# Score tiles set apart, q and k turned together, and x of batch 3 turned by transfers, in a kernel of attention and an MLP

## The chip, the cores and the metric

The kernel runs on one core of one Trainium2 chip. The metric is device time in microseconds (us); three runs of the kernel before took 359.74, 359.81 and 360.06 us, median 359.81. The engines are named as in the profile: PE is the matrix engine, PEld its weight loads, DVE the vector engine, ACT the scalar engine with its activation functions, POOL the general-purpose engine, SP the engine that only issues transfers here.

## What is computed

The reference is attention with a decay ("forgetting attention"), followed by an MLP. There are 8 batches of 8 heads; a sequence has 576 positions and a head 64 elements.

```python
scores = scale * np.matmul(q, k.transpose(0, 1, 3, 2))
cum = np.cumsum(np.log(np.clip(f, 0.0001, 1.0)), axis=-1)
scores = np.where(causal, -1e9, scores + cum[..., :, None] - cum[..., None, :])
attn = softmax(scores)                       # over the last axis
x = np.matmul(attn, v)                       # then (B, S, H*D) -> 4608 x 512
h = x @ w_in                                 # 512 x 2048
out = (h * 1 / (1 + np.exp(-h))) @ w_out     # 2048 x 512
```

Inputs and output are float32; the matrix products run in bfloat16.

## The kernel before, in words

**Attention.** A *pair* is two heads of one batch; there are four pairs per batch and 32 in all, numbered p = 0 to 31. `scores(p, t)` makes one of four tiles (t = 0 to 3) of the transposed scores of a pair: keys on the partitions, queries along the row, only the part at or below the diagonal. Both heads use 64 rows of PE each (64 is the head's size). A score tile `sc` lies in one of two PSUM buffers; ACT takes the exponential of it into `uT`. The diagonal blocks must be masked. In the first four pairs a large negative number is added to the score tile before the exponential, by DVE, or for tile 2 by PE; later DVE multiplies the exponentials with zeros and ones. The decay does not enter the scores: v, and a column of ones beside it, are multiplied by `wT`, a function of the running sum of log f, by POOL in `prep_v` (result `vaug`, three buffers). `attend_rows(p)` multiplies `uT` with `vaug` on PE (30 matmuls of 65 columns, called row sums in this text), and DVE divides by the column that sums the weights (`rr`, `xt`).

**Getting q and k to lie with the head's elements on the partitions.** Batches 0 and 1, and q of batch 2, come as float32 (`whole`, `raw`), are cast by POOL (`cast_both`), transposed by PE (`transposes`, tile `tpqk`) and copied by DVE. Everything later is loaded by POOL's queue with a cast (`load_qk`, tile `mp`), one block of 128 positions of q or k at a time, and transposed by a transfer issued on SP (`turn_qk`).

**Turning x.** The MLP needs x with its 512 columns on the partitions. For batches below `NTURN` = 4, `turn_pair` transposes a pair's x on PE (five transposes, tile `tpx`; the last has 64 rows) and ACT copies it to `xT` (two copies per pair). For the other batches `retire` puts five turns of a whole block by transfer (`turn_batch`, on SP) on a list, due 2.5 to 7.3 units of the planner's clock later.

**The MLP.** Tokens are taken in nine groups of 512. `m1_chunk` makes a 128-row slice of the first layer (four matmuls of 512 columns, tile `hp`), then ACT's tanh (`th`) and DVE's product (`gtile`), 16 per group. `m2_part` is a quarter of an output tile of the second layer (four matmuls, tile `po`); the fourth quarter is followed by ACT's copy (`osb`) and a store. These chunks and parts are called parts below. Part n of an output tile reads the n-th quarter of w_out, and the four quarters are loaded by POOL in this order after `prep_v` of pair 4.

**What sets the order.** Every engine runs its instructions in the order in which this Python code issues them. A loop over pairs 4 to 31 issues each pair's scores, the row sums of the pair before, loads and turns by a table (`plan`, `fetch`), and n parts, given by `pace`: what is ready, spread over the pairs until the next group will be ready, with `LAG` (10) in units of time for the wait at the batch's end and at most `MOST` = 9. `work(n)` takes parts from the two queues; `spend` moves the planner's clock, and what was put off with `defer` is issued when the clock has passed its time. Before pair 4 the order is written out by hand; after pair 31 the rest of the MLP follows without a pause.

The lines that matter below are 270 to 320 (`scores`), 337 to 377 (row sums and turns of x by PE), 379 to 438 (turns by transfer, the MLP), 484 to 539 (pace, retire, tables) and 594 to 701 (the order by hand and the loop).

Of the kernel before, what the change touches and what calls it, by code (L numbers as in the profile page):

```python
# [13 lines left out]
FP32 = mybir.dt.float32  # L14
BF16 = mybir.dt.bfloat16
P = 128
# [3 lines left out]
def kernel(  # L20
# [29 lines left out]

    const = ctx.enter_context(tc.tile_pool(name="const", bufs=1))
    ident_bf = const.tile([P, P], BF16, name="ident_bf")
    ident_f = const.tile([P, P], FP32, name="ident_f")
# [6 lines left out]
    vaugs = [const.tile([P, NB, 2, DV], BF16, name=f"vaug{i}") for i in range(NVA)]  # L60
    kTs = [const.tile([P, NPB, NB * P], BF16, name=f"kT{i}") for i in range(2)]
# [3 lines left out]
    qkp = ctx.enter_context(tc.tile_pool(name="qkp", bufs=2))  # L65
    vp = ctx.enter_context(tc.tile_pool(name="vp", bufs=2))
# [8 lines left out]
    RAW = {0: (0, 1), 1: (0, 1), 2: (0,)}  # L75
    NTURN = 4
    LAG = 10.0
    MOST = 9.0
# [5 lines left out]
    def qk_tiles(b):  # L84
        qkT[b] = (qkp.tile([P, NPB, S], BF16, name="qT", tag="qT"), kTs[b % 2])

# [36 lines left out]
    def load_qk(b, c, which):  # L123
        t = sbp.tile([P, DM], BF16, name="mp", tag="mp", bufs=16)
        raw[b, c, which] = t
        nc.gpsimd.dma_start(  # L126
            out=t[: bs[c], :].rearrange("p (h d) -> p h d", h=H),
            in_=(q, k)[which][b, :, c * P : c * P + bs[c], :].rearrange("h p d -> p h d"),
        )

    def turn_qk(b, c, which):
        if b not in qkT:
            qk_tiles(b)
        n = bs[c]
        nc.sync.dma_start_transpose(
            out=qkT[b][which][:, :, c * P : c * P + n], in_=raw[b, c, which][:n, :]
        )
# [16 lines left out]
    def decay_sum():  # L154
        lnf = f_sb
        cum = evp.tile([BH, S], FP32, name="cum", tag="ev")
        nc.vector.tensor_tensor_scan(
            out=cum[:, :], data0=lnf[:, :], data1=lnf[:, :], initial=0.0,
            op0=ALU.add, op1=ALU.bypass,
        )  # L160
        mid = const.tile([BH, 1], FP32, name="mid")
        nc.vector.tensor_scalar_mul(out=mid[:, :], in0=cum[:, S - 1 : S], scalar1=0.5)
        cumc = cum
        nc.vector.tensor_scalar(
            out=cumc[:, :], in0=cum[:, :], scalar1=mid[:, 0:1], scalar2=None,
            op0=ALU.subtract,
        )
        cums.append(cumc)

    cums: list = []  # L170
# [35 lines left out]
    def turn_first(which):  # L206
        qk_tiles(0) if 0 not in qkT else None
        m = cast[0, 0, which].rearrange("p c h d -> p c (h d)")
        tp = big([P, SM], BF16, "tpqk")
        for c in range(NB - 1):  # L210
            nc.tensor.transpose(tp[:, c * P : (c + 1) * P], m[:, c, :], ident_bf[:, :])
        nc.vector.tensor_copy(
            out=qkT[0][which][:, 0, 0:SM].rearrange("x (p c) -> x p c", c=NB - 1),
            in_=tp[:, :].rearrange("x (c p) -> x p c", c=NB - 1),
        )

# [53 lines left out]
    def scores(p, t):  # L270
        qT, kT = (x[:, p % NPB, :] for x in qkT[p // NPB])
        u = us[p % 3]
        first = p < NPB
        sc = psc.tile([P, 2, 512], FP32, name="sc", tag="sc")
# [209 lines left out]
    def pace(p):  # L484
        b, j = divmod(p, NPB)
        if b < NEARLY:
            return have() / (NPB - j)
        for b in range(B):
            if (b + 1) * S // TG > m1_ready:
                break  # L490
        n = MOST
        for _ in range(20):
            k = NPB * (b + 1) - p + min(LAG, 3.5 * (b - 1)) / (2.3 + 0.88 * n)
            n = 0.5 * n + 0.5 * have() / max(k, 1.0)
        return min(n, MOST)
# [10 lines left out]
    def retire(p):  # L506
# [3 lines left out]
        for c in range(NB):  # L510
            defer(2.5 + 1.2 * c, lambda c=c: turn_batch(b, c))
        for g in range(b * S // TG, (b + 1) * S // TG):
# [10 lines left out]
    for b in range(NEARLY, B):  # L523
        for i, group in enumerate([(0, 1), (2,), (3, 4)]):
            at = NPB * b - 4 + min(i, 1) if b == NEARLY else NPB * b - 7 + i
            late = 1 if b == NEARLY + 1 and len(RAW[NEARLY]) == 2 else 0
            for c in group:
                for w in range(2):
                    if w in RAW.get(b, ()):
                        continue  # L530
                    add(fetch, at + late, load_qk, b, c, w)
                    if b <= NEARLY + 1:
                        to = min(at + late + (2 if b == NEARLY else 3), NPB * b - 2)
                        add(plan, to, turn_qk, b, c, w)
                    elif i == 0 and b - 2 >= NTURN:
                        add(plan, NPB * b - 4, defer, 9.0, partial(turn_qk, b, c, w))
                    else:
                        add(plan, NPB * b - 4 + min(i, 1), turn_qk, b, c, w)
                add(plan, NPB * b - 5 + i + (b == NEARLY), load_v, b, c, nc.sync)
# [11 lines left out]

    with tc.manual_schedule():
        nc.scalar.dma_start(out=f_sb[:, :], in_=f.rearrange("b h s -> (b h) s"))
        load_main(0, 0, 2)
# [17 lines left out]
        make_identity(nc, ident_f)  # L572
        for kT in kTs:
            nc.vector.memset(kT[:, :, S:], 0.0)
        for u in us:
# [17 lines left out]
        load_w(w_in_bf, moe_w_in, DFF // 2, DFF)  # L593
        for w in range(2):
            turn_first(w)
        scores(0, 0)
        turn_first_tails()
        scores(0, 1)
        decay_sum()
        scores(0, 3)  # L600
        transposes(1, 0)
        scores(0, 2)
        decay_turn()
        prep_v(0)
        transposes(1, 1)
        scores(1, 0)
        cast_both(3)
        load_tail(1)
# [4 lines left out]
        for p in range(1, NPB):  # L613
# [3 lines left out]
            if more:  # L617
                transposes(p + 1, 0)
            scores(p, 3)
            if more:  # L620
                transposes(p + 1, 1)
            if p > 1:
                turn_pair(p - 2)
            attend_rows(p - 1, LO)
            scores(p, 2)
# [20 lines left out]
        for p in range(NPB, NP):  # L646
# [6 lines left out]
            due -= n  # L653
            n1, n2 = (n + 2) // 3, (n + 1) // 3
            n3 = n - n1 - n2
            scores(p, 0)
            scores(p, 1)
            spend(0.4)
            work(n1)
            ahead = RAW.get((p + 1) // NPB, ())  # L660
            rows = NPB < p < NPB * NEARLY
            if 0 in ahead:
                transposes(p + 1, 0)
# [71 lines left out]
```

## Time and profile before

| | |
|---|---|
| three runs | 359.74, 359.81, 360.06 us |
| profiled execution | 359.25 us, of which the profile's span is 357.5 |
| PE | 336.3 us busy, 94% |
| ACT | 211.9 us, 59% |
| DVE | 191.7 us, 54% |
| POOL | 119.6 us, 33% |
| first layer (`hp`) | 135.8 us of PE, second layer (`po`) 133.7 |
| row sums (`avr`) | 36.2 us of PE, 960 matmuls |
| scores (`sc`) | 37.3 us of PE, 384 matmuls, 2 to 8 at a time |
| x transposed by PE (`tpx`) | 64 matmuls of 128 rows and 16 of 64 |

The page has the busy time of each engine, rows of 40 slices of the span, the queues, the chain of work that ended last, and the costliest groups with what ended the idle time before them. A timeline's line gives start, duration, engine, source line, operation, tiles and count; where there was an idle time before it of which the end is known, it stands in brackets with its releaser. A matmul's duration is longer than its place in the stream, since matmuls overlap; what a step costs is read from starts. The table by stretch gives the length of the stretch, busy time and count of PE, PEld, DVE, ACT and POOL, the granted clock, the share of the transfer engines, and GB/s. Some matmul records are missing, so a count can be one or two too low.

### The profile page before, as it was taken

The page shows a single profiled execution, that of the slowest core. Times are in us where ns is not written, and L with a number is a line of the kernel's source. Part 1 is how long each engine was busy: PE and PEld are TensorE (multiplying, and loading weights), DVE is VectorE, ACT ScalarE, POOL GpSimd, SP SyncE. Part 2 cuts the span into 40 slices and gives each one's busy share as a digit, 9 for nine tenths or more (in the row PEclk, how much of TensorE's full clock was granted, in tenths as well). Part 3 has the DMA queues.
Part 4 walks back from the last instruction along what each step waited for, and adds up shares of the span by engine and source line. Part 5 has one row for each costly group of instructions (what it writes and reads, how often), then busy time and mean ns, then how long its engine had stood idle before and what let it go on. Part 6 is the DMA issues. An engine that isn't in the chain of part 4 may idle for free.

```text
span 357.5 us, 7026 instructions
## 1 busy us (share of the span) xinstructions
PE 336.3 (94%) x2656; PEld 168.4 (47%) x2697; DVE 191.7 (54%) x450; ACT 211.9 (59%) x345; POOL 119.6 (33%) x207
## 2 busy tenths in 40 slices
PE   2797989999999999999999999999999999999995
PEld 1455445554555445544454453444444454444442
DVE  4664895538743675348543791567237723744300
ACT  4566674558753986388647764676468615644421
POOL 5563598239554235423564250110301000000000
PEclk9999999999999999999999999999999999999999
DMA  8899999999997998399969994452240014000021
GB/s 220 213 208 315 192 193 222 155 210 170 148 150 117 163 150 78 89 170 142 124 122 152 130 166 123 100 117 75 74 83 31 1 68 118 2 29 29 31 76 71
DMA packets 142514, 44.92 MB, mean 126 GB/s; under 512 B 129616, under 2 KB 136784, under 8 KB 142480
## 3 DMA queue, kind: packets, MB, share of 16 engines
q1 hardware_dynamic: 87664, 33.64, 42.5%
q0 software_dynamic: 54736, 10.69, 38.4%
q8 instruction: 21, 0.34, 0.4%
q10 hardware_dynamic: 80, 0.15, 0.2%
q14 instruction: 13, 0.11, 0.1%
HBM read 36.85 MB, written 9.44 MB: 129 GB/s over the span
## 4 chain that ended last, share of the span: by engine, by line
PE 82%; DVE 6%; ACT 4%; DMA 3%; issue 3%; POOL 1%; SPq 0%; ACTq 0%
PE po L425 33%; PE hp L400 30%; PE avr L349 7%; PE sc L281 7%; DVE gtile L412 2%; ACT uT L306 2%; DMA xT<-xt 2%; PE tpx L371 2%; DVE uT L320 2%; PE tpqk L235 2%; ACT th L411 1%; DMA whole<-in_k_dram 1%; DVE xt L359 1%; PE sc L289 1%; DVE qT L240 1%
## 5 line engine op out<-in xcount | busy, mean ns | idle before, releaser
L400 PE MATMUL hp<-xT,w_in_bf 128*128 128x512 bf16 x556 | 135.8, 380 | 3.2 <-DVE gtile L412 0.8
L425 PE MATMUL po<-w_out_bf,gtile 128*128 128x512 bf16 x555 | 133.7, 379 | 1.4 <-DVE gtile L412 0.4
L412 DVE SCALAR_TENSOR_TENSOR gtile<-th,hp 128x512 bf16<-128x512 bf16 x144 | 96.0, 685 | 52.2 <-ACT th L411 50.3
L306 ACT ACTIVATE uT<-sc 128x1024 bf16<-128x1024 f32 (+1 forms) x128 | 101.3, 850 | 24.9 <-PE sc L281 15.9
L411 ACT ACTIVATE th<-hp 128x512 bf16<-128x512 f32 x144 | 84.8, 613 | 50.0 <-PE hp L400 46.2
L251 POOL TENSOR_TENSOR vaug<-vm,wT 128x512 bf16<-128x512 f32 x64 | 45.4, 729 | 132.7 <-PE avr L349 121.4
L400 PEld LDWEIGHTS <-w_in_bf 128*128 128x128 bf16 x576 | 53.1, 98 | 65.2 <-issue 6.1
L425 PEld LDWEIGHTS <-gtile 128*128 128x128 bf16 x576 | 53.6, 98 | 62.9 <-issue 2.4
L320 DVE TENSOR_TENSOR uT<-uT,mask 128x256 bf16<-128x256 bf16 (+1 forms) x112 | 35.3, 337 | 66.2 <-ACT uT L306 66.0
L434 ACT ACTIVATE osb<-po 128x512 f32<-128x512 f32 x36 | 21.7, 602 | 46.7 <-PE po L425 46.7
L281 PE MATMUL sc<-qT,kT 64*128 64x64 bf16 (+4 forms) x384 | 37.3, 287 | 5.5 <-ACT uT L306 2.2
L349 PEld LDWEIGHTS <-uT 128*128 128x128 bf16 x960 | 33.7, 98 | 6.4 <-issue 0.7
L349 PE MATMUL avr<-vaug,uT 128*128 128x65 bf16 x960 | 36.2, 195 | 0.2 <-POOL vaug L259 0.2
L359 DVE TENSOR_TENSOR xt<-avr,rr 128x384 bf16<-128x384 f32 x64 | 31.4, 491 | 2.3
L281 PEld LDWEIGHTS <-kT 64*128 64x128 bf16 x384 | 15.3, 95 | 30.1 <-issue 21.0
L126 POOL DMA_DIRECT2D mp<-in_k_dram x30 | 25.9, 865 | 1.0 <-DMA mp<-in_k_dram 1.0
L126 POOL DMA_DIRECT2D mp<-in_q_dram x25 | 22.2, 887 | 1.3 <-DMA w_out_bf<-in_moe_w_out_dram 0.5
L358 DVE RECIPROCAL rr<-avr 128x6 f32<-128x6 f32 x64 | 11.7, 183 | 18.6 <-PE avr L349 18.5
L377 ACT COPY xT<-tpx 128x512 bf16<-128x512 bf16 (+7 forms) x32 | 11.2, 404 | 17.0 <-PE tpx L371 16.9
L193 POOL CAST m<-whole 128x512 bf16<-128x512 f32 x20 | 11.9, 607 | 15.0 <-DMA whole<-in_q_dram 12.4
L235 PE MATMUL tpqk<-ident_bf,m 128*128 128x128 bf16 (+1 forms) x90 | 10.9, 241 | 0.3 <-DVE gtile L412 0.3
L235 PEld LDWEIGHTS <-m 128*128 128x128 bf16 (+1 forms) x90 | 7.3, 106 | 6.3 <-issue 1.6
(47 smaller groups left out, 71.8 us busy)
## 6 DMA issues: line engine op xcount, KB each, us to landing
out_dram<-osb SPq DMA_DIRECT2D x36, 256.0 KB, 2.2
vm<-in_v_dram SPq DMA_DIRECT2D x32, 256.0 KB, 4.7
mp<-in_k_dram POOLq DMA_DIRECT2D x24, 128.0 KB, 6.2
whole<-in_q_dram SPq DMA_DIRECT2D x5, 512.0 KB, 9.7
mp<-in_q_dram POOLq DMA_DIRECT2D x20, 128.0 KB, 4.8
w_in_bf<-in_moe_w_in_dram POOLq DMA_DIRECT2D x2, 1024.0 KB, 11.2
w_out_bf<-in_moe_w_out_dram POOLq DMA_DIRECT2D x4, 512.0 KB, 10.7
whole<-in_k_dram SPq DMA_DIRECT2D x3, 512.0 KB, 9.5
```

Of the source, the lines that this page charges most:

```text
L126: nc.gpsimd.dma_start(out=t[: bs[c], :].rearrange("p (h d) -> p h d", h=H), in_=(q, k)[which][b, :, c * P : c * P + bs[c], :].rearrange("h ...
L235: nc.tensor.transpose(tp[:, c * P : c * P + n], m[:n, c, :, :].rearrange("p h d -> p (h d)"), ident_bf[:n, :n],)
L251: nc.gpsimd.tensor_tensor(out=va[:n, c0:c1, :, 0:D], in0=vm[:n, c0:c1, 2 * j : 2 * j + 2, :], in1=wT[:n, c0:c1, 2 * j + b * H : 2 * j + 2 ...
L281: nc.tensor.matmul(sc[:, i, col : col + n], lhsT=kT[r, kb * P : (kb + 1) * P], rhs=qT[r, q0 : q0 + n], start=True, stop=not pe_adds,)
L306: nc.scalar.activation(out=u[:, :, o : o + col], in_=sc[:, :, 0:col], func=ACT.Exp, scale=scale)
L320: nc.vector.tensor_tensor(out=d, in0=d, in1=mk, op=ALU.mult)
L349: nc.tensor.matmul(av[:, qb - lo, i, :], lhsT=u[:, i, o : o + P], rhs=va[:, kb, i, :], start=(kb == 0), stop=(kb == qb),)
L359: nc.vector.tensor_tensor(out=xt[:, lo:hi, 2 * j : 2 * j + 2, :], in0=av[:, :, :, 0:D], in1=r[:, 0:n, :, None].to_broadcast([P, n, 2, D]), ...
L400: nc.tensor.matmul(hp[:, :], lhsT=w_in_bf[:, cc, fc * P : (fc + 1) * P], rhs=xg[g][:, cc, :], start=(cc == 0), stop=(cc == NCC - 1),)
L411: nc.scalar.activation(out=th[:, :], in_=hp[:, :], func=ACT.Tanh, scale=0.5)
L412: nc.vector.scalar_tensor_tensor(out=gte[:, fc, :], in0=th[:, :], scalar=1.0, in1=hp[:, :], op0=ALU.add, op1=ALU.mult,)
L425: nc.tensor.matmul(po[:, :], lhsT=gte[:, fc, tb * P : (tb + 1) * P], rhs=w_out_bf[:, fc, :], start=(fc == 0), stop=(fc == NFC - 1),)
```

## The change

1. `scores` adds the mask before the exponential in pairs 4 and 5 too, except in tile 2.
2. In the loop, the parts of a pair stand in other places: in batches 1 and 2 some stand between any two of the four score tiles; later two tiles still follow each other, with a third of the parts behind the first two. (`step` keeps the count.)
3. q and k of a batch share one buffer, and one transfer turns a block of both (8 x 128 columns where there were two of 4 x 128). The loads of a block of q and k share one tile, of which there are eight.
4. x of batch 3 is turned by transfers (`NTURN` 3), and the turns of a batch are issued at once behind its last row sums, ahead of what SP is given next.
5. `LAG` is 14, and from the batch at which transfers begin it is no longer shortened, so more parts are kept for the wait at a batch's end.
6. Ahead of the row sums of pair 0, 34 matmuls of a zero tile (`spin`) stand between PE's other work; the first copy of k is made in two pieces.

```diff
-    NTURN = 4
-    LAG = 10.0
+    NTURN = 3
+    LAG = 14.0
...
-    def turn_qk(b, c, which):
+    def turn_qk(b, c):
...
         nc.sync.dma_start_transpose(
-            out=qkT[b][which][:, :, c * P : c * P + n], in_=raw[b, c, which][:n, :]
+            out=qkTs[b % 2][:, w[0] :, :, c * P : c * P + n].rearrange(
+                "x w j n -> x (w j) n"
+            ),
+            in_=raw[b, c][:n, w[0] * DM :],
         )
...
+    def spin(n):
+        ps = big([P, SM], FP32, "spin")
+        for _ in range(n):
+            nc.tensor.matmul(
+                ps[:, :], lhsT=idle[:, 0:P], rhs=idle[:, :], start=True, stop=True
+            )
...
-        nc.vector.tensor_copy(
-            out=qkT[0][which][:, 0, 0:SM].rearrange("x (p c) -> x p c", c=NB - 1),
-            in_=tp[:, :].rearrange("x (c p) -> x p c", c=NB - 1),
-        )
+        dst = qkT[0][which][:, 0, 0:SM].rearrange("x (p c) -> x p c", c=NB - 1)
+        for p0, p1 in ((0, P),) if which == 0 else ((0, P // 4), (P // 4, P)):
+            nc.vector.tensor_copy(
+                out=dst[:, p0:p1, :],
+                in_=tp[:, :].rearrange("x (c p) -> x p c", c=NB - 1)[:, p0:p1, :],
+            )
...
-        first = p < NPB
+        first = p < NPB + 2 and (t != 2 or p < NPB)
...
-            k = NPB * (b + 1) - p + min(LAG, 3.5 * (b - 1)) / (2.3 + 0.88 * n)
+            k = NPB * (b + 1) - p + (LAG if b >= NTURN else min(LAG, 3.5 * (b - 1))) / (2.3 + 0.88 * n)
...
         for c in range(NB):
-            defer(2.5 + 1.2 * c, lambda c=c: turn_batch(b, c))
+            turn_batch(b, c)
...
-        for w in range(2):
-            turn_first(w)
+        spin(7)
+        turn_first(0)
+        spin(4)
+        turn_first(1)
+        spin(2)
         scores(0, 0)
         turn_first_tails()
+        spin(2)
         scores(0, 1)
+        spin(3)
...
-            n1, n2 = (n + 2) // 3, (n + 1) // 3
-            n3 = n - n1 - n2
-            scores(p, 0)
-            scores(p, 1)
-            spend(0.4)
-            work(n1)
+            scores(p, 0)
+            spend(0.3)
+            step(0.2 if b <= NEARLY else 0.0)
+            scores(p, 1)
+            spend(0.3)
+            step(0.2 if b <= NEARLY else 0.35)
...
-            if early:
-                work(n2 // 2)
+            step(0.1 if b <= NEARLY else 0.0)
             scores(p, 2)
+            spend(0.3)
+            step(0.2 if b <= NEARLY else 0.0)
             scores(p, 3)
-            spend(0.3)
+            spend(0.2)
...
+            step(0.1)
             if rows:
                 attend_rows(p - 1, HI)
-            work(n2 - n2 // 2 if early else n2)
+            step(0.0 if b <= NEARLY else 0.25)
             if b >= NEARLY and j > 0:
                 attend_rows(p - 1)
                 spend(1.2)
-            work(n3)
+            work(left)
```

More of the change, by code (lines that the diff above doesn't have):

```diff
@@ L51 @@
     const = ctx.enter_context(tc.tile_pool(name="const", bufs=1))
+    idle = const.tile([P, SM], BF16, name="idle")
     ident_bf = const.tile([P, P], BF16, name="ident_bf")
@@ L60 @@
     vaugs = [const.tile([P, NB, 2, DV], BF16, name=f"vaug{i}") for i in range(NVA)]
-    kTs = [const.tile([P, NPB, NB * P], BF16, name=f"kT{i}") for i in range(2)]
+    qkTs = [const.tile([P, 2, NPB, NB * P], BF16, name=f"qkT{i}") for i in range(2)]
     us = [const.tile([P, 2, UW], BF16, name=f"uT{i}") for i in range(3)]
     xp = ctx.enter_context(tc.tile_pool(name="xp", bufs=4))
-    qkp = ctx.enter_context(tc.tile_pool(name="qkp", bufs=2))
     vp = ctx.enter_context(tc.tile_pool(name="vp", bufs=2))
@@ L84, in qk_tiles @@
     def qk_tiles(b):
-        qkT[b] = (qkp.tile([P, NPB, S], BF16, name="qT", tag="qT"), kTs[b % 2])
+        qkT[b] = (qkTs[b % 2][:, 0], qkTs[b % 2][:, 1])
     def raw_tile():
@@ L123, in load_qk @@
     def load_qk(b, c, which):
-        t = sbp.tile([P, DM], BF16, name="mp", tag="mp", bufs=16)
-        raw[b, c, which] = t
+        if (b, c) not in raw:
+            raw[b, c] = sbp.tile([P, 2 * DM], BF16, name="mp", tag="mp", bufs=8)
         nc.gpsimd.dma_start(
-            out=t[: bs[c], :].rearrange("p (h d) -> p h d", h=H),
+            out=raw[b, c][: bs[c], which * DM : (which + 1) * DM].rearrange(
+                "p (h d) -> p h d", h=H
+            ),
             in_=(q, k)[which][b, :, c * P : c * P + bs[c], :].rearrange("h p d -> p h d"),
         )
-    def turn_qk(b, c, which):
+    def turn_qk(b, c):
         if b not in qkT:
@@ L134, in turn_qk @@
         n = bs[c]
+        w = [x for x in range(2) if x not in RAW.get(b, ())]
         nc.sync.dma_start_transpose(
-            out=qkT[b][which][:, :, c * P : c * P + n], in_=raw[b, c, which][:n, :]
+            out=qkTs[b % 2][:, w[0] :, :, c * P : c * P + n].rearrange(
+                "x w j n -> x (w j) n"
+            ),
+            in_=raw[b, c][:n, w[0] * DM :],
         )
@@ L528 @@
                 for w in range(2):
[L529 to L538, printed above, removed]
+                    if w not in RAW.get(b, ()):
+                        add(fetch, at + late, load_qk, b, c, w)
+                if b <= NEARLY + 1:
+                    to = min(at + late + (2 if b == NEARLY else 3), NPB * b - 2)
+                else:
+                    to = NPB * b - 4 + min(i, 1)
+                add(plan, to, turn_qk, b, c)
                 add(plan, NPB * b - 5 + i + (b == NEARLY), load_v, b, c, nc.sync)
@@ L552 @@
     with tc.manual_schedule():
+        nc.vector.memset(idle[:, :], 0.0)
         nc.scalar.dma_start(out=f_sb[:, :], in_=f.rearrange("b h s -> (b h) s"))
@@ L572 @@
         make_identity(nc, ident_f)
-        for kT in kTs:
-            nc.vector.memset(kT[:, :, S:], 0.0)
+        for t in qkTs:
+            nc.vector.memset(t[:, 1, :, S:], 0.0)
         for u in us:
@@ L593 @@
         load_w(w_in_bf, moe_w_in, DFF // 2, DFF)
-        for w in range(2):
-            turn_first(w)
+        spin(7)
[3 more added lines that the diff above has]
+        spin(2)
         scores(0, 0)
         turn_first_tails()
+        spin(2)
         scores(0, 1)
+        spin(3)
         decay_sum()
         scores(0, 3)
+        spin(1)
         transposes(1, 0)
+        spin(2)
         scores(0, 2)
+        spin(1)
         decay_turn()
@@ L605 @@
         transposes(1, 1)
+        spin(4)
         scores(1, 0)
+        spin(2)
         cast_both(3)
@@ L618 @@
                 transposes(p + 1, 0)
+            if p == 1:
+                spin(2)
             scores(p, 3)
@@ L623 @@
                 turn_pair(p - 2)
+            else:
+                spin(4)
             attend_rows(p - 1, LO)
@@ L653, with step @@
             due -= n
-            n1, n2 = (n + 2) // 3, (n + 1) // 3
-            n3 = n - n1 - n2
-            scores(p, 0)
-            scores(p, 1)
-            spend(0.4)
-            work(n1)
             ahead = RAW.get((p + 1) // NPB, ())
             rows = NPB < p < NPB * NEARLY
+            left, part = n, 0.0
+            def step(share):
+                nonlocal left, part
+                part += share * n
+                k = min(left, int(part + 0.5))
+                part -= k
+                left -= k
+                work(k)
+            scores(p, 0)
[4 more added lines that the diff above has]
+            step(0.2 if b <= NEARLY else 0.35)
             if 0 in ahead:
```

## The prediction

> **What bounds the kernel now.** I read the page first: TensorE (PE) is busy 94% of a span of 357.5 us, and the chain that ended last is 82% PE. Then the busy time by stretch, to see where the other 6% lies.
>
> ```profile
> PE 336.3 (94%) x2656; PEld 168.4 (47%) x2697; DVE 191.7 (54%) x450; ACT 211.9 (59%) x345; POOL 119.6 (33%) x207
> DMA  8899999999997998399969994452240014000021
> ```
> ```profile
> 0.00:35.00 35.00, 24.20 (x256) 14.40 (x258) 19.39 (x58) 19.74 (x30) 18.95 (x47) 1.00 0.99 238
> 35.00:57.50 22.50, 20.55 (x151) 10.17 (x152) 19.71 (x39) 14.71 (x24) 17.49 (x31) 1.00 1.19 194
> 57.50:100.00 42.50, 40.98 (x360) 21.49 (x365) 25.36 (x63) 28.47 (x49) 23.00 (x37) 1.00 1.66 177
> 150.00:340.00 190.00, 187.75 (x1377) 90.37 (x1398) 100.99 (x223) 115.18 (x184) 38.54 (x62) 1.00 0.55 90
> ```
>
> PE idles 10.8 us of the first 35, 2.0 of the next 22.5, and then 4.5 up to 340. The second line is the DMA row: nine tenths and more from the second slice to past 60 us, so the front is paced by transfers too. Behind 57 us there is little waiting to win, and what an edit adds to PE's stream is paid almost in full.
>
> Two lines of the front matter: when POOL issued the w_out loads, and when PE used them (timelines of POOL and PE; then landings of the issue at 43.6, with its neighbour).
>
> ```profile
> 39.85 1.40 POOL L251 TENSOR_TENSOR vaug<-vm,wT 128x512 bf16<-128x512 f32 x2 [4.49 <-DMA vm<-in_v_dram]
> 41.33 3.03 POOL L542 DMA_DIRECT2D w_out_bf<-in_moe_w_out_dram  x4
> 57.33 0.88 POOL L126 DMA_DIRECT2D mp<-in_q_dram  x1 [0.52 <-DMA w_out_bf<-in_moe_w_out_dram]
> ...
> 56.12 2.76 PE L425 MATMUL po<-w_out_bf,gtile 128*128 128x512 bf16 x12
> ...
> DMA to landing us min/median/max: 11.7/12.6/13.5
> ```
>
> The fourth load, issued at 43.6, lands 13.5 us later, at 57.1; POOL, which waits for that queue, goes on at 57.33. PE starts the part that reads it eight matmuls into the last PE line: 56.12 + 8 x 0.216 = 57.85. So only about 0.6 us lies between landing and use.
>
> Third, what a step in PE's stream costs (PE timeline in four narrow windows).
>
> ```profile
> 116.62 0.38 PE L400 MATMUL hp<-xT,w_in_bf 128*128 128x512 bf16 x1
> 116.84 0.38 PE L425 MATMUL po<-w_out_bf,gtile 128*128 128x512 bf16 x1
> ...
> 118.35 0.38 PE L400 MATMUL hp<-xT,w_in_bf 128*128 128x512 bf16 x1
> 118.66 0.31 PE L281 MATMUL sc<-qT,kT 64*128 64x320 bf16 x2
> ...
> 150.74 0.52 PE L371 MATMUL tpx<-ident_bf,xt 128*128 128x128 bf16 x5
> 151.06 0.63 PE L281 MATMUL sc<-qT,kT 64*128 64x512 bf16 x6
> ```
>
> From one 128-row matmul to the next the starts lie 0.22 apart (hp to po), but from a 128-row matmul to a 64-row score matmul 0.31. A change of row count costs 0.10, as long as the score's weight load (95 ns in its group). Leaving costs the same: the last 64-column score pair to the next hp takes 0.12, where pairs inside follow within 0.03. Five transposes of a pair end in a 64-row one, so scores behind them pay nothing more: tpx to sc is 0.32.
>
> **The change part by part.** An "MLP part" is four matmuls, 4 x 0.216 = 0.865.
>
> Front (spins, the k copy in two, the memset). 34 spin matmuls stand ahead of the first row sums, seven of them in the 4.51 us before PE's first work. Five transposes took 0.78 at 16.79 and 0.52 at 38.65, a ratio of 0.67, though the granted clock reads 1.00 in both. If the spins bring the quick matmuls on early, the other 27 cost 5.8 us, against 4.25 of waits between 4.51 and 17.74 and a third (2.9) off the 8.6 us of work there: they fit. If they don't, they cost 27 x 0.216 x 1.5 = 8.8, or 4.5 us too much. I take the first, since PE became fast at 22 after 4.2 us without a gap. The Trainium skill, "TensorE: Matmul & The Clock Gate", Part 1, says that an idle array runs at half rate and is released after about 3.4 us of activity; no run here yet shows it for spins. Row sums of pair 0 still wait for POOL's vaug (17.69), which hangs on transfers alone. From there to 21.98 the sluggish matmuls took 4.24 us; a third off gives 1.4. The split copy (0.18 for 64 columns, 0.69 for 512; I take 0.3 for its first piece) and the memset (0.17 to 0.33 on an idle DVE) lie ahead of that wait and count nothing.
>
> Masks of pairs 4 and 5 added before the exponential. Two masks of pair 4 took 2.09 beside a busy POOL, the adds cost 0.43 each and 0.28 for the small one; DVE's queue then lets kT go sooner. Of the 1.95 us that PE idles from 35 to 57.5 I count 1.7 as gone (bounds 0 and 1.95). Setting score tiles apart adds eight changes of row count in pairs 4 and 5, 0.8. So PE would reach that last w_out part 1.4 + 1.7 - 0.8 = 2.3 us sooner, at 55.55. But the load lands at 57.1 to 57.3: its issue hangs on prep_v(4), that on the v loads at 39.85, those on transfers and POOL, none of them changed. PE waits, and **0.6** is what remains.
>
> Score tiles set apart in pairs 6 to 11. Counted in the order of both built programs, changes of row count in these pairs go from 34 to 64: two more places per pair where parts stand between two tiles, and transposes that led straight into scores now lead into a part. 30 x 0.096 = **+2.9**, all on PE, in a stretch where PE waited 1.5 us. Later pairs keep two tiles together and gain none.
>
> The Trainium skill, same page, "Step-by-step: what each phase is for", has PE pull weight loads ahead of running matmuls when row groups don't conflict or a background buffer takes them, and gives 128 columns / 1.2 GHz = 107 ns for one. An estimate by that price is 3.2 instead of 2.9; an estimate by the pulling ahead is nothing, the first rival below. The trace agrees with the pulling ahead from 128 rows to 128 rows (0.22) and not from 128 to 64 (0.31).
>
> Batch 3's x turned by transfers. Four times five transposes go: three that led into scores save 0.32 - 0.10 = 0.22 each, one that led into row sums 0.45 (147.64 to 148.09): **-1.1**. ACT loses eight copies of 0.40, beside PE. SP gains six turns of 1.24; group 3 needs three of them, so 3 x 1.24 + 2.4 to 4.9 landing = 6.1 to 8.6 after the last row sums. Cover: seven MLP parts (6.05), two pairs' scores (1.9), one pair's row sums (0.9) = 8.9. Hidden; if that cover is gone, each late us costs one.
>
> x turns at once, q and k together. Turns stand ahead of the next q/k turns, v loads and output stores on SP, which wait up to 1 us for DVE plus 6.2 us of issue; four osb buffers cover two stores. The q/k issues go from 55 to 30; the wide one costs between 1.2 and 2.4 us of SP, I take 1.9, a batch ahead of use: nothing. At groups 4 and 5 PE had waited 0.3 and 0.3 for xT; the turns now start some 3 us sooner, -0.6. POOL's loads wait for q/k turns of one batch earlier (eight double buffers for sixteen): those landed before 75, hidden.
>
> Waits otherwise. The 0.44 for gtile at 85.68 goes with parts spread finer, -0.4. Pair 12 now has four first-layer parts and one second-layer part: ACT 3 x 1.03 + 0.30 + 4 x 0.61 + 0.60 = 6.4 against PE's 5.4; before, 7.7 against 7.2. Scores of pair 13 wait for it: +0.6 beside the 0.33 at 128.43. Transposes of pairs 6, 9 and 10 have one part (0.865) between row sums and themselves where there were two or three; with none, at 76.86, PE waited 0.55, so +0.4 in all. The 0.52 for an exponential at 191.61 (a pair with one part) moves to pair 17. Net 0; bounds -1 to +1.5.
>
> Sum: -0.6 + 2.9 - 1.1 + 0 = +1.2. The profiled execution took 359.25 (span 357.5 and 1.75 around it), which gives 360.45; the median of the runs shown is 359.81, 0.56 above it, so **361.0**.
>
> **The rivals.**
> - Changes of row count cost nothing when a part stands between tiles, because the score weights are loaded while the part runs. For it: 128-row loads are hidden that way. The Trainium skill's sentence on weight loads, above, would allow it too. Against it: every hp or po to sc step I read is 0.31. Price: the 2.9 goes, 359.81 - 1.7 = 358.1. It decides if a change costs under 0.03; above 0.08 the kernel is slower.
> - The load wall doesn't stand: w_out lands 2 us sooner and 2.3 instead of 0.6 come through, 359.81 - 0.5 = 359.3. Against it: a DMA row at nine tenths up to there, and unchanged queues.
> - Waits grow: ACT binds in pairs 12 to 14 and the transposes wait for DVE in each early pair, +1.5: 362.5. For it: ACT's 6.4 against 5.4.
> - Spins change nothing in that: 4.5 late and the 1.4 not gained; 4.5 - 1.7 + 0.8 = 3.6 late past the wall, with +1.8 behind it 365.2. Against it: 22 us.
>
> **How the numbers follow.** Forecast 0.50 (own range 360.2 to 361.9), row changes free 0.12, no wall 0.14, waits grow 0.17, spins in vain 0.07. About 0.2% (0.7 us) is what a measurement can tell from no change: faster is under 359.1, slower over 360.5. Faster: free changes 0.12 and most of no wall 0.08, 0.20. Same: the rest of no wall and the forecast's lower end, 0.18. Slower 0.62. The range leaves out the free changes and the vain spins: 359.0 to 362.9.
>
> **What the profile after would show.** Transposes at 0.52 for five from before 10 us; row sums of pair 0 still at about 17.7; a PE wait on w_out near 55 to 57; hp to sc still 0.31, and pair 8 to 11 longer by 0.4 to 0.6 each; no tpx after pair 11; hp of group 3 without a wait for xT. Wrong would be: no wait on w_out, score tiles entered at 0.22, or PE idling over 1 us in pairs 12 to 17.

## The result, and the profile after

The changed kernel took 362.61 us (median of six runs, 362.28 to 364.40); the kernel before, run beside it, took 359.77 (six runs, 359.22 to 360.87). The ratio is 1.0084, with a 95% interval of 1.0059 to 1.0109: slower by about 3 us. The profiled execution took 362.71 us, of which the span is 360.5; the prediction's sum for it was 360.45.

The page of the changed kernel: PE is busy for longer, and one slice has a clock below full.

```profile
PE 344.7 (96%) x2668; PEld 166.3 (46%) x2711; DVE 192.4 (53%) x452; ACT 209.6 (58%) x337; POOL 120.3 (33%) x207
PEclk9999989999999999999999999999999999999999
```

Busy time says little here, since matmuls at half the clock count as busy (1.71 of the 2.00 us from 50 on, below), and the spins count too. What tells is where each pair's first score tile starts on PE. All columns but the first are differences to it, from one profiled execution of each kernel; e1 to e11 are the experiments below.

| start of | before, us | after | e1 | e2 | e3 | e4 | e6 | e8 | e9 | e11 |
|---|---|---|---|---|---|---|---|---|---|---|
| pair 4 | 42.26 | -1.88 | -2.23 | -1.80 | -2.26 | -1.58 | -0.58 | -0.71 | -1.83 | -0.73 |
| pair 5 | 50.16 | +0.13 | -2.25 | -1.56 | -2.71 | -0.50 | -0.46 | -0.51 | -2.11 | +1.55 |
| pair 6 | 59.04 | +1.41 | -1.09 | +1.40 | -1.32 | -0.50 | -0.46 | +0.91 | -0.88 | +2.95 |
| pair 12 | 115.40 | +4.52 | +2.00 | +1.08 | -1.44 | -0.45 | +0.04 | +1.11 | +2.21 | +6.04 |
| PE's end | 353.54 | +3.31 | +0.77 | -0.16 | -2.66 | +0.11 | -1.36 | +0.98 | +1.04 | +5.97 |

The column "after" splits the result in four: the front gains 1.88, pairs 4 and 5 lose 3.29, pairs 6 to 11 lose 3.11, and from pair 12 to the end 1.21 are won. The sum on record was -0.6 at pair 6, +2.9 to pair 12, -1.1 behind it. So the miss is one place, pairs 4 and 5. Single executions vary, though: e6, e8 and e11 have no spins and still start pair 4 0.58 to 0.73 sooner than this execution of the kernel before, so a difference of that size at pairs 4 to 6 says nothing by itself.

*Front.* In PE's timeline of the changed kernel, five transposes take 0.53 at 12.34, where before they took 0.78 at 16.79 still, and the row sums of pair 0 start at 17.68, as the prediction had it, right behind POOL's vaug (17.63). The first two lines below are of the kernel before, where the matmuls are still slow at 21.98 and quick at 24.05; the others are of the changed kernel.

```profile
21.98 0.77 PE L235 MATMUL tpqk<-ident_bf,m 128*128 128x128 bf16 x5
24.05 0.54 PE L349 MATMUL avr<-vaug,uT 128*128 128x65 bf16 x12
...
12.34 0.53 PE L250 MATMUL tpqk<-ident_bf,m 128*128 128x128 bf16 x5
...
16.55 1.04 PE L179 MATMUL spin<-idle 128*128 128x512 bf16 x4
17.68 0.52 PE L364 MATMUL avr<-vaug,uT 128*128 128x65 bf16 x12
```

The granted clock reads 1.00 in the table by stretch all this while, but the trace has no clock record ahead of 23.77 us in the kernel before and 5.63 in the changed one, which is where the matmuls become quick in each. So the 1.00 of the early stretches is no reading.

*Pairs 4 and 5.* ACT's timeline in pair 4 of the kernel before (first line: two exponentials right behind each other) and of the changed kernel, then DVE's of the changed kernel:

```profile
42.86 1.94 ACT L306 ACTIVATE uT<-sc 128x1024 bf16<-128x1024 f32 x2
...
42.19 1.02 ACT L321 ACTIVATE uT<-sc 128x1024 bf16<-128x1024 f32 x1 [1.10 <-DVE sc L315]
43.11 0.59 ACT L426 ACTIVATE th<-hp 128x512 bf16<-128x512 f32 x1
44.80 1.03 ACT L321 ACTIVATE uT<-sc 128x1024 bf16<-128x1024 f32 x1 [1.10 <-DVE sc L315]
```
```profile
41.73 0.43 DVE L315 TENSOR_TENSOR sc<-sc,maskadd 128x256 f32<-128x256 f32 x1
43.73 0.69 DVE L427 SCALAR_TENSOR_TENSOR gtile<-th,hp 128x512 bf16<-128x512 bf16 x1 [1.58 <-ACT th L426]
44.34 0.43 DVE L315 TENSOR_TENSOR sc<-sc,maskadd 128x256 f32<-128x256 f32 x1
46.34 0.69 DVE L427 SCALAR_TENSOR_TENSOR gtile<-th,hp 128x512 bf16<-128x512 bf16 x1 [1.58 <-ACT th L426]
```

Read the two together as a ring. ACT's exponential (42.19) waits for DVE's add (41.73 to 42.16). The tanh (43.11) stands behind the exponential in ACT's queue, so it can't start earlier. DVE's gtile (43.73) waits for that tanh, and the next add (44.34) stands behind gtile in DVE's queue. The next exponential (44.80) waits for that add. One round takes 44.80 - 42.19 = 2.61 us for one exponential and one tanh, which ACT alone would do in 1.6. ACT and DVE take turns, and each idles while the other works. PE then waits in its own timeline for gtile and for the copies of q and k that stand in DVE's queue:

```profile
47.08 0.52 PE L250 MATMUL tpqk<-ident_bf,m 128*128 128x128 bf16 x5 [1.01 <-DVE gtile L427]
47.79 1.04 PE L415 MATMUL hp<-xT,w_in_bf 128*128 128x512 bf16 x4 [0.19 <-DVE qkT L259]
50.29 0.61 PE L296 MATMUL sc<-qkT 64*128 64x512 bf16 x2 [1.47 <-DVE qkT L255]
50.84 1.89 PE L415 MATMUL hp<-xT,w_in_bf 128*128 128x512 bf16 x4
```

The last line has four matmuls in 1.89 where 47.79 has them in 1.04: the clock has fallen. The table by stretch shows it as 0.50 and 0.64 (after the length of the stretch come busy time and count of PE, PEld, DVE, ACT and POOL, the granted clock, the share of the transfer engines, and GB/s):

```profile
50.00:52.00 2.00, 1.71 (x5) 0.54 (x6) 1.37 (x4) 0.90 (x2) 2.00 (x5) 0.50 1.24 206
52.00:54.00 2.00, 1.75 (x9) 0.51 (x9) 0.55 (x1) 1.17 (x2) 2.00 (x5) 0.64 1.24 206
```

*Pairs 6 to 11.* A score tile between two parts, in PE's timeline: 112.71 + 4 x 0.216 would be 113.57 for the next 128-row matmul, and 113.68 is where the score starts; from there it takes 0.13 to be out again.

```profile
112.71 1.04 PE L440 MATMUL po<-w_out_bf,gtile 128*128 128x512 bf16 x4
113.68 0.20 PE L296 MATMUL sc<-qkT 64*128 64x64 bf16 x2
113.81 1.04 PE L440 MATMUL po<-w_out_bf,gtile 128*128 128x512 bf16 x4
```

*w_out.* The landings of its four loads, of which POOL issued the last at 44.1:

```profile
DMA to landing us min/median/max: 5.8/9.1/11.7
```

They are all in by 55.8, and PE starts the last quarter of its first output tile only at 59.26. The wait that the prediction named isn't there, because PE came late.

### The profile page after: what moved, and what is told of

Read it like the earlier page. It is cut to its first block, busy times and chain, and to the rows that moved or that the text cites. A ratio compares the mean times of both kernels' runs of the same rounds, so it can differ in the third digit from the quotient of the medians.

```text
span 360.5 us, 7019 instructions
## 1 busy us (share of the span) xinstructions
PE 344.7 (96%) x2668; PEld 166.3 (46%) x2711; DVE 192.4 (53%) x452; ACT 209.6 (58%) x337; POOL 120.3 (33%) x207
## 4 chain that ended last, share of the span: by engine, by line
PE 84%; ACT 5%; DVE 4%; issue 3%; DMA 2%; SPq 1%; POOL 1%; ACTq 0%
PE po L440 34%; PE hp L415 32%; PE sc L296 7%; PE avr L364 7%; ACT uT L321 3%; ACT th L426 2%; PE tpqk L250 2%; DMA whole<-in_k_dram 1%; PE tpx L386 1%; DVE gtile L427 1%; DVE xt L374 1%; DMA vm<-in_v_dram 1%; PE spin L179 1%; DVE uT L335 1%; PE sc L304 0%
## 5 line engine op out<-in xcount | busy, mean ns | idle before, releaser
L415 PE MATMUL hp<-xT,w_in_bf 128*128 128x512 bf16 x556 | 139.4, 382 | 3.1 <-ACT xT L392 0.7
L440 PE MATMUL po<-w_out_bf,gtile 128*128 128x512 bf16 x554 | 136.5, 380 | 1.2 <-issue 0.2
L321 ACT ACTIVATE uT<-sc 128x1024 bf16<-128x1024 f32 (+1 forms) x128 | 102.6, 849 | 37.7 <-PE sc L296 22.8
L440 PEld LDWEIGHTS <-gtile 128*128 128x128 bf16 x576 | 52.4, 98 | 61.4 <-issue 4.3
L335 DVE TENSOR_TENSOR uT<-uT,mask 128x512 bf16<-128x512 bf16 (+1 forms) x106 | 33.3, 331 | 57.6 <-ACT uT L321 57.1
L296 PE MATMUL sc<-qkT 64*128 64x64 bf16 (+4 forms) x384 | 38.7, 281 | 3.3 <-DVE qkT L255 1.5
L296 PEld LDWEIGHTS <-qkT 64*128 64x128 bf16 x384 | 14.8, 94 | 37.7 <-issue 29.1
L392 ACT COPY xT<-tpx 128x512 bf16<-128x512 bf16 (+5 forms) x24 | 8.4, 405 | 13.2 <-PE tpx L386 13.2
L255 DVE COPY qkT<-tpqk 128x512 bf16<-128x512 bf16 x18 | 12.3, 683 | 1.7 <-PE tpqk L250 1.6
L179 PE MATMUL spin<-idle 128*128 128x512 bf16 x33 | 11.3, 452 | 1.2 <-DVE idle L565 1.2
```

The source lines that it names most:

```text
L296: nc.tensor.matmul(sc[:, i, col : col + n], lhsT=kT[r, kb * P : (kb + 1) * P], rhs=qT[r, q0 : q0 + n], start=True, stop=not pe_adds,)
L321: nc.scalar.activation(out=u[:, :, o : o + col], in_=sc[:, :, 0:col], func=ACT.Exp, scale=scale)
L335: nc.vector.tensor_tensor(out=d, in0=d, in1=mk, op=ALU.mult)
L415: nc.tensor.matmul(hp[:, :], lhsT=w_in_bf[:, cc, fc * P : (fc + 1) * P], rhs=xg[g][:, cc, :], start=(cc == 0), stop=(cc == NCC - 1),)
L440: nc.tensor.matmul(po[:, :], lhsT=gte[:, fc, tb * P : (tb + 1) * P], rhs=w_out_bf[:, fc, :], start=(fc == 0), stop=(fc == NFC - 1),)
```

## The experiments

Each experiment is compared with the kernel before on its own chip, whose medians were 359.17 (e1, e2, e3, e7), 359.12 (e4, e5, e6, e8) and 359.21 us (e9, e10, e11). Where an expectation goes by 359.8 or 362.6, the kernel before was thus some 0.6 us faster on the experiment's chip.

### e1: the masks of pairs 4 and 5 back behind the exponential

```diff
-        first = p < NPB + 2 and (t != 2 or p < NPB)
+        first = p < NPB
```

> The changed kernel with the masks of pairs 4 and 5 multiplied in behind the exponential again; all else as changed. My theory: the added masks make ACT and DVE take turns in pairs 4 and 5 (exponential waits for the add, the add stands behind gtile, gtile waits for th, th stands behind the exponential), and that costs PE some 3 us there. Then PE's idle between 40 and 56 us falls from 4.5 to under 2, no stretch has a granted clock under 1.00, the last part of the first output tile starts at 57.2 to 57.8 instead of 59.3 (w_out lands then), and the time is 360.5 to 361.2 against 362.6. Rival, the score tiles set apart cause the waits in pairs 4 and 5 too: the time stays above 362.0 and ACT still idles in front of the exponentials there.

Measured: 360.04 us (359.49 to 361.69), ratio 1.0036 (1.0021 to 1.0052). Pairs 4 and 5 now lose 1.14 instead of 3.29, and the wait for w_out stands where the prediction had put it (PE's timeline):

```profile
56.76 1.02 PE L440 MATMUL po<-w_out_bf,gtile 128*128 128x512 bf16 x3 [1.01 <-DMA w_out_bf<-in_moe_w_out_dram]
```

So most of the 1.14 is that wall. The time is 0.5 under the expected 360.5, about as much as the chips differ.

### e2: the parts of batches 1 and 2 placed as before

The masks stay ahead of the exponential; `first_way` works off a given count of parts.

```diff
+            n1, n2 = (n + 2) // 3, (n + 1) // 3
...
-            step(0.2 if b <= NEARLY else 0.0)
+            step(0.0)
...
-            step(0.2 if b <= NEARLY else 0.35)
+            first_way(n1) if old else step(0.35)
...
-            step(0.2 if b <= NEARLY else 0.0)
+            step(0.0)
```

> The changed kernel with the parts of batches 1 and 2 where they stood before, so that two score tiles follow each other; masks still added in pairs 4 and 5. My theory: 38 changes of row count go (30 of them in pairs 6 to 11), at 0.096 us each, so the time falls by 2.9 to 3.6, to 359.0 to 359.7, and the distance from the start of pair 6 to that of pair 12 falls from 59.5 to 56.4 as before. Rival, the waits of pairs 6 to 11 (transposes with one part of cover) and not the row count are what was lost: the steps from a 128-row matmul to a score matmul stay 0.31, but the distance falls by under 1.

Measured: 359.07 us (358.37 to 360.28), ratio 1.0000 (0.9986 to 1.0014). From pair 6 to pair 12 it takes 56.04 us where the changed kernel takes 59.47: 3.4 for the 30 changes of row count and what hangs on them. But pair 6 is as late as in the changed kernel (+1.40), with tiles together: what pairs 4 and 5 lose isn't the tiles set apart. (About 1.1 of that is a stretch at half the clock in this execution: at 56.44 twelve matmuls of the second layer take 3.83, and 2.76 in the kernel before at 56.12.) PE's longest wait there is again for gtile:

```profile
53.65 1.02 PE L440 MATMUL po<-w_out_bf,gtile 128*128 128x512 bf16 x3 [1.78 <-DVE gtile L427]
```

### e3: both of these

```diff
-        first = p < NPB + 2 and (t != 2 or p < NPB)
+        first = p < NPB
...
+            n1, n2 = (n + 2) // 3, (n + 1) // 3
+            n3 = n - n1 - n2
...
-            step(0.2 if b <= NEARLY else 0.35)
+            first_way(n1) if old else step(0.35)
```

> The changed kernel with both undone: masks as before, parts of batches 1 and 2 as before. What is left of the change: spins, wide turns, x of batch 3 by transfer, turns at once, more work kept back. My theory: the front arrives 1.9 us sooner at the MLP, but the wait for w_out leaves 0.3 to 0.8 of it; the turns of x give 1.1 to 1.3; so 357.6 to 358.4 against 359.8 before. Rival, w_out doesn't bind: the 1.9 come through too, 356.5 to 357.0. Rival, the wide turns or the turns at once cost something: not under 359.3.

Measured: 356.90 us (356.72 to 357.74), ratio 0.9948 (0.9928 to 0.9968): faster than the kernel before. Pair 5 starts 2.71 sooner, pair 6 only 1.32, and what lies between is in PE's timeline:

```profile
56.54 1.02 PE L440 MATMUL po<-w_out_bf,gtile 128*128 128x512 bf16 x4 [0.92 <-DMA w_out_bf<-in_moe_w_out_dram]
```

The time lies in the range of the rival in which w_out doesn't bind, but 0.6 of that is the chip, and the wait is there. So the wall is shown, but not its height. The prediction took the landing of the kernel before, 57.1; here PE goes on at 56.54, and 1.3 came through and not 0.6. Against e6, which has no spins and stands at -0.46 at pair 6, it is 0.9.

### e8: the masks ahead of the exponential, alone on the kernel before

```diff
-        first = p < NPB
+        first = p < NPB + 2 and (t != 2 or p < NPB)
```

> The kernel before with the masks of tiles 0, 1 and 3 of pairs 4 and 5 added before the exponential, and nothing else. Theory (the add stands between PE's score tile and ACT's exponential, so ACT and DVE take turns, and PE waits for gtile and for q and k): pairs 4 and 5 together are 2.5 to 3.2 us longer, a stretch of 2 us with a granted clock near 0.5 stands close behind pair 5, and the time is 361.6 to 362.4 against 359.2. Rival (the add is harmless by itself and costs only when PE comes early from a quicker front): pairs 4 and 5 within 0.6 us of before, 358.9 to 359.8.

Measured: 361.12 us (359.84 to 362.27), ratio 1.0046 (1.0027 to 1.0065), 2.0 us slower. The profiled execution lies low in its runs (360.25) and loses 1.6 from pair 4 to pair 6. The wait is the same:

```profile
54.70 1.02 PE L425 MATMUL po<-w_out_bf,gtile 128*128 128x512 bf16 x3 [1.78 <-DVE gtile L412]
```

No stretch of this execution from 35 to 57.5 us has a clock below 1.00, so the ring costs without the clock. The theory held in kind: PE waits for gtile as in the changed kernel. But its size was too high, 2.0 where 2.4 to 3.2 was expected, and the stretch at half the clock that it expected didn't come in this execution.

### e9: the same masks ahead of the exponential, but added by PE

```diff
-        pe_adds = adds if first and t == 2 else []
+        pe_adds = adds if first and (t == 2 or p >= NPB) else []
...
-                    stop=not pe_adds,
+                    stop=not (pe_adds and q0 == kb * P),
...
-            for i in range(2) if pe_adds else ():
+            w = min(n, P)
+            for i in range(2) if pe_adds and q0 == kb * P else ():
...
-                    sc[:, i, col : col + P],
+                    sc[:, i, col : col + w],
...
-                    rhs=maskadd[:, :],
+                    rhs=maskadd[:, 0:w],
```

> The changed kernel, with the masks of tiles 0, 1 and 3 of pairs 4 and 5 still added before the exponential, but by PE as an identity times the mask behind the scores, so that DVE has no part between the score tile and ACT. Six more matmuls of 64 to 128 columns per pair. Theory (what costs pairs 4 and 5 the 3.3 us is that ACT and DVE take turns): ACT's waits for the add go, pairs 4 and 5 are 2 to 3 us shorter than in the changed kernel, w_out's wait comes back near 56.5, and the time is 360.0 to 361.0, as with the masks behind the exponential (360.0). Rival (it lies in the mask standing ahead of the exponential at all, or in thinner PE work and its clock): 362.0 or more, with PE waits for gtile as before.

Measured: 359.65 us (359.05 to 360.89), ratio 1.0012 (0.9998 to 1.0026); 362.61 against 359.77 had been 2.84 slower, this is 0.44. ACT's timeline, to be held against the one above:

```profile
41.08 1.02 ACT L322 ACTIVATE uT<-sc 128x1024 bf16<-128x1024 f32 x1
42.00 0.59 ACT L427 ACTIVATE th<-hp 128x512 bf16<-128x512 f32 x1
42.48 1.02 ACT L322 ACTIVATE uT<-sc 128x1024 bf16<-128x1024 f32 x1
```

Two exponentials lie 1.40 apart where they lay 2.61, with no wait. The mask stands ahead of the exponential in both, the parts stand apart in both; only the engine that adds differs. That settles it: the loss is DVE's place between the score tile and ACT. The wait for w_out is back (0.89 at 56.97).

### e4: the front alone on the kernel before

The zero tile, its memset, the 34 spins and nothing else; the first copy of k stays whole, although the expectation names it.

```diff
+    idle = const.tile([P, SM], BF16, name="idle")
...
+        nc.vector.memset(idle[:, :], 0.0)
...
-        for w in range(2):
-            turn_first(w)
+        spin(7)
+        turn_first(0)
+        spin(4)
+        turn_first(1)
+        spin(2)
         scores(0, 0)
         turn_first_tails()
+        spin(2)
         scores(0, 1)
+        spin(3)
...
```

> The kernel before with the front of the change alone: the zero tile, the 34 spins and the first copy of k in two pieces. Theory (the front makes PE early by about 1.9 us at pair 4, and the last part of w_out takes some of that back): pair 4 starts 1.7 to 2.3 us sooner than before, a wait on w_out of 0.7 to 1.3 us stands near 56.5, and 0.6 to 1.3 us remain at pair 6 and at the end, 357.8 to 358.6 against 359.2. Rival one (no wall): 1.8 to 2.3 us remain, under 357.4. Rival two (the front is worth something only with the other edits): 359.0 or more.

Measured: 358.40 us (357.41 to 359.79), ratio 0.9980 (0.9960 to 1.0001): inside the expected 357.8 to 358.6, but not apart from no change. The profiled execution took 359.38 and keeps 0.5 of the 1.58 that it has won at pair 4. The expected wait for w_out isn't there, so something else takes the rest. DVE's and POOL's timelines, and a wait of PE that follows:

```profile
42.33 2.82 DVE L328 TENSOR_TENSOR uT<-uT,mask 128x256 bf16<-128x256 bf16 x2 [0.23 <-ACT uT L314]
```
```profile
43.90 1.51 POOL L259 TENSOR_TENSOR vaug<-vm,wT 128x512 bf16<-128x512 f32 x2
```
```profile
49.66 0.61 PE L289 MATMUL sc<-qT,kT 64*128 64x512 bf16 x6 [1.37 <-DVE kT L248]
```

Two mask multiplications took 2.82, up to 45.15, while POOL's products ran from 43.90 to 45.41; the two of e3, which were done at 43.2, ahead of POOL's product at 44.38, took 0.29 and 0.63. So it may be that how much of the front comes through depends on whether the second multiplication of pair 4 gets ahead of that product. This is read from two traces and was not tested by itself.

### e11: the changed kernel without its spins

```diff
-        spin(7)
         turn_first(0)
-        spin(4)
         turn_first(1)
-        spin(2)
         scores(0, 0)
         turn_first_tails()
-        spin(2)
         scores(0, 1)
-        spin(3)
...
```

> The changed kernel without the 34 spin matmuls; all else of it stays. Theory (pairs 4 and 5 are so slow in the changed kernel that w_out has landed when PE comes to it, so the whole gain of the front comes through there): pair 4 starts 1.5 to 2.0 us later than in the changed kernel, pair 6 too, and the time is 363.8 to 364.6 against 362.6. Rival (the prediction's term: most of the front's gain is lost again by pair 6): pair 6 starts at most 0.7 us later, 362.5 to 363.2.

Measured: 365.61 us (365.24 to 366.35), ratio 1.0184 (1.0168 to 1.0199). Pair 4 starts 1.15 later than in the changed kernel, less than the 1.5 to 2.0 expected, and pair 6 1.54, so in that kernel the whole gain of the front comes through, as the theory has it. The time is 1.0 us above the theory's end: another 1.15 come at pair 20, where PE waits for x turned by a transfer (PE's timeline, then SP's).

```profile
190.34 1.04 PE L415 MATMUL hp<-xT,w_in_bf 128*128 128x512 bf16 x4 [0.99 <-DMA xT<-xt]
```
```profile
182.51 7.35 SPq L397 DMA_TRANSPOSE xT<-xt  x5
```

In the changed kernel these five took 6.52 and no wait follows. Why they take longer without spins is open.

### e5: e3 with the w_out loads issued ahead of prep_v(4)

```diff
-        prep_v(NPB)
         for c in range(0, NFC, NFC // 4):
             load_rows(w_out_bf, moe_w_out, c, c + NFC // 4)
+        prep_v(NPB)
```

> The change without its masks and without tiles set apart in batches 1 and 2 (356.9 us in an earlier run), and the four w_out loads issued by the general-purpose engine ahead of the values of pair 4 instead of behind them, about 4 us sooner. Theory (that last load is what takes back part of the front's gain): it lands before 55.5, the wait of 0.9 us at 56.5 goes, pair 6 starts 0.8 to 1.2 us sooner, and the time is 355.7 to 356.2. Rival (the transfer engines are full up to there, so the load lands no sooner or the values of batch 1 come later by as much): 356.6 or more, with the wait still there or another for vaug in pairs 4 and 5.

Measured: 362.11 us (358.96 to 363.20), ratio 1.0060 (1.0032 to 1.0089). The wait for w_out is gone, and a worse one stands in its place (POOL's timeline, then PE's):

```profile
35.62 3.04 POOL L554 DMA_DIRECT2D w_out_bf<-in_moe_w_out_dram  x4
47.68 1.05 POOL L266 TENSOR_TENSOR vaug<-vm,wT 128x512 bf16<-128x512 f32 x1 [9.01 <-PE sc L296]
51.08 0.40 POOL L266 TENSOR_TENSOR vaug<-vm,wT 64x128 bf16<-64x128 f32 x1 [2.35 <-DMA vm<-in_v_dram]
```
```profile
53.71 0.40 PE L250 MATMUL tpqk<-ident_bf,m 128*128 128x128 bf16 x4 [4.24 <-POOL m L206]
```

The values of batch 1 are complete only at 51.08, where e3's POOL went on with them at 39.87. (The releaser named for 47.68, a score of PE, is no input of that product, so the 9.01 us too are put down to those transfers by inference.) POOL stands still, its casts of pair 6 come late, and PE idles 4.24 us. The transfer engines were full, as the rival said (this run's DMA row is at nine tenths up to 54 us): the load that was moved ahead was paid by another.

### e7: tiles set apart in batches 3 to 7 too

```diff
-            step(0.2 if b <= NEARLY else 0.0)
+            step(0.2)
...
-            step(0.2 if b <= NEARLY else 0.35)
+            step(0.2)
```

> The changed kernel with the four score tiles set apart in batches 3 to 7 too (the shares of batches 1 and 2 for all). A price by itself: 76 changes of row count more, in the order of the built program. If each costs PE 0.096 us, the time grows by 7.3 less what waits it fills, to 368.5 to 370; the masks and the front are the same in both. Rival, a part between two tiles hides the weight load of the next, and what batches 1 and 2 lose are waits of their own: under 364.

Measured: 369.32 us (368.78 to 369.97), ratio 1.0287 (1.0268 to 1.0305). Against the changed kernel that is 6.7 us, or 7.3 by the two ratios, for 76 more changes: 0.09 to 0.10 each. From pair 21 to pair 31 each pair is longer by 0.42 to 0.43.

### e6: x of batch 3 turned by transfers, with the new pace, alone on the kernel before

```diff
-    NTURN = 4
-    LAG = 10.0
+    NTURN = 3
+    LAG = 14.0
...
-            k = NPB * (b + 1) - p + min(LAG, 3.5 * (b - 1)) / (2.3 + 0.88 * n)
+            k = NPB * (b + 1) - p + (LAG if b >= NTURN else min(LAG, 3.5 * (b - 1))) / (2.3 + 0.88 * n)
...
-            defer(2.5 + 1.2 * c, lambda c=c: turn_batch(b, c))
+            turn_batch(b, c)
...
```

> The kernel before with x of batch 3 turned by transfers, a batch's x turns issued at once, and the new pace, alone; q and k of a block are still turned apart. Theory (20 transposes off PE in batch 3, the transfers hidden behind kept-back MLP work): 1.1 to 1.5 us less from pair 12 to the end and nothing changed ahead of it, 357.7 to 358.2 against 359.2. Rival (a wait for xT of group 3 or for q and k turned apart takes the place): PE waits of 0.5 us or more in pairs 16 to 18, and 358.7 or more.

Measured: 357.90 us (357.75 to 358.10), ratio 0.9956 (0.9939 to 0.9973), 1.2 us less. Between 118 and 160 us PE waits at most 0.52 us at once, and never for xT.

### e10: e3 with x of batch 2 turned by transfers as well

```diff
-    NTURN = 3
+    NTURN = 2
```

> The change without its masks and without tiles set apart in batches 1 and 2 (356.9 us in an earlier run), with x of batch 2 turned by transfers too: 20 more transposes and eight copies by ACT go. Theory (a batch's transposes are worth 1.1 us of PE, and its transfers are hidden where MLP work is kept back): 355.6 to 356.1. Rival (batch 2 has less work in hand, and its six turns share SP and the transfer engines with loads that fill them to nine tenths up to 60 us and more; PE waits for xT of group 2 at the end of pair 11): 356.7 or more, with PE waits over 1 us near 110 us.

Measured: 356.50 us (355.81 to 356.95), ratio 0.9927 (0.9909 to 0.9945), the fastest kernel here, 2.7 us ahead of the one before. Against e3 it is 0.4 us by the medians and 0.8 by the two ratios, between the two theories: no wait for xT comes near 110 us (the second line is group 2's first part, in PE's timeline; the first is SP's), but PE's end is only 0.43 sooner.

```profile
106.17 6.54 SPq L397 DMA_TRANSPOSE xT<-xt  x5
```
```profile
116.42 1.03 PE L415 MATMUL hp<-xT,w_in_bf 128*128 128x512 bf16 x3
```

## Why the prediction was right, and where it was wrong

The time, 362.61, lies inside the stated range and on the side that had 0.62, but 1.6 above the 361.0 and outside the forecast's own 360.2 to 361.9. That the stated range holds it is in part luck: it reaches up to 362.9 for the rival of growing waits, which didn't act where it was put. Of the forecast's own signs of being wrong, one came: no wait on w_out. By its steps:

- **"Front": right in mechanism, and in size as far as can be told.** Spins make the matmuls quick, and the row sums of pair 0 still wait for POOL. The matmuls that the prediction counted took 4.24 us before (17.74 to 21.98) and take 2.83 after (17.68 to 20.51), which is the forecast 1.4. It ended the slow stretch too early: PE wasn't fast at 22 but between 22.74, where five transposes still take 0.78, and 24.05. So 1.7 is won by the first transposes of x (23.44 before, 21.70 after). The 1.88 at pair 4 is 1.15 against e11. The Trainium skill, "TensorE: Matmul & The Clock Gate", Part 1, speaks of the release of an idle array after about 3.4 us of activity: the trace agrees, also for matmuls of a zero tile (the first spin starts at 1.20; four transposes take 0.61 at 4.28 and 0.39 at 6.02).
- **"Of the 1.95 us that PE idles from 35 to 57.5 I count 1.7 as gone (bounds 0 and 1.95)": this is the step that failed.** The price of the adds was compared with that of the multiplications, and who waits for them was left out. A multiplication behind the exponential has row sums waiting, a pair later, and what stands behind it in DVE's queue; an add ahead of it holds ACT's exponential too, and in ACT's queue the tanh behind that, and in DVE's queue the gtile behind that. Pairs 4 and 5 lost 3.29 where the prediction, ahead of the wait for w_out, had them win 0.9. How the 3.29 divides isn't shown: eight changes of row count are in it (0.8 by the prediction's own count), the half clock behind 50 us, and the ring, which e8 prices at 2.0 alone and e2 against e3 at 2.2, where -1.7 had been put. e9 shows the cause. Its bounds were wrong too: no reason had excluded a loss.
- **"PE waits, and 0.6 is what remains": right in mechanism, hidden by the miss.** e1, e3 and e9 show the wait, 0.89 to 1.01 us long. In the changed kernel PE came after the load, so the wall stood 3.5 us ahead of it (55.8 against 59.26). The remainder in e3 is 1.3, or 0.9 against e6, since PE goes on at 56.54.
- **"30 x 0.096 = +2.9": right.** Pairs 6 to 11 took 3.11 more, 3.4 between e2 and the changed kernel, and e7 gives 0.09 to 0.10 for a change. So the rival of free changes falls, and with it the pulling ahead of weight loads, which the Trainium skill (same page, "Step-by-step: what each phase is for") would allow where row groups don't conflict or a background buffer takes the load: score tiles are still entered 0.31 after the last part's matmul. The record of weight loads (PEld) of the changed kernel shows it: a load between two 128-row matmuls starts at 113.15, a whole matmul ahead of the one that uses it (113.37), and the score's starts at 113.67, with its own matmul (113.68).
- **"-1.1" for batch 3's x: right.** 1.21 from pair 12 to the end, 1.2 in e6 alone. The wait for an exponential moved to pair 17, as named: 0.52 at 156.92.
- **"Net 0" for other waits:** pairs 12 to 14 didn't become longer by ACT; from 119 to 160 us PE's longest wait is the 0.52 named above. The rival "waits grow" gave 362.5, nearly the time that came, but its waits were in the wrong place; the number is no support for it.
- **A reading that changed nothing:** the DMA row is at nine tenths from the third slice (18 us) on, not from the second.

## What to carry to other kernels

When an operation is moved ahead of another engine's, don't compare durations alone: write down both engines' queues for one round and look for a ring, in which each engine's next item waits for the other's last. A gain in front of a stage counts only up to the next transfer that the stage needs (e1, e3, e9), and while the transfer engines are full, a load moved sooner can take its time from another (e5). On PE, count the places where 64-row and 128-row matmuls meet; each cost about 0.1 us here, with parts of 0.865 us between them. And compare single executions with several of the other kernel before reading a few tenths from them.

## What the runs showed of the hardware that was not expected

**The clock falls without a long gap.** Between 45.87 and 50.29 us the changed kernel's PE waits 1.01, 0.19 and 1.47 us with three short runs of matmuls between (starts 45.87, 47.08, 47.79, lengths 0.20, 0.52, 1.04), and from 50 us on the granted clock reads 0.50. The Trainium skill, "TensorE: Matmul & The Clock Gate", "Why this matters for your kernels", asks for no idle gap over about 3 us; no single gap here is half of that, so this trace differs. Its section "A second HAM failure mode: psum-queue depth-cycling" tells of frequent small idles doing the same, and this trace is of that kind. How much idling is enough is open: e8's PE waits 0.88, 0.62 and 1.78 us between 46 and 55 us, and its clock stays at 1.00 there. The cost varies: of the six runs of the changed kernel, two had a mean clock of 0.999 and took 362.28 and 362.39, three had 0.995 and took 362.50 to 362.95, and one had 0.988 and took 364.40.

**A DVE multiplication of two SBUF tiles can take several times as long beside POOL's work.** 2.82 us for two in e4 against 0.29 + 0.63 in e3. The second of e4's two took 1.91, and POOL multiplied for most of it; the first took 0.90, while POOL was issuing the loads of w_out, so the product alone doesn't explain it. The Trainium skill, "SBUF — State Buffer", "Who interferes with whom", says that a DVE instruction with two SBUF inputs contends with a POOL instruction that reads SBUF; these traces agree. The add ahead of the exponential has its score tile in PSUM, and took 0.43 in the lines shown. So the move of the mask avoided long multiplications of DVE and made ACT wait.
